# An attention and mixture-of-experts kernel: scores by pairs of key blocks with half passes, and some loads and stores begun by another engine

## The chip, the cores and the metric

The kernel runs on one core of a Trainium2 chip. The core has five engines that run their own instruction lists in order: TensorE (PE in the rows; its weight loads are listed as PEld), VectorE (DVE), ScalarE (ACT), GpSimd (POOL) and SyncE (SP), which here only begins DMA transfers. The metric is the device time of one execution in microseconds (us); smaller is better. For the kernel before, the median of three runs is 4315.48 us (4313.22 to 4316.8).

## The reference

Eight samples of 3072 rows go through three steps:

```
scores = z @ z.T / S                       # z: 3072 x 64 for each sample
out    = u * (max(scores, 0) ** 2 @ v)     # v, u: 3072 x 256
h      = out @ w_in                        # 24576 rows, 256 -> 1024
ln     = layernorm(h * softmax(h)) * g_ln
x      = ln @ w_out                        # 1024 -> 256
e      = argmax(x @ w_gate)                # one of 8 experts for each row
y      = gate * (max(x @ w1[e], 0) @ w2[e])
```

All of it is wanted in float32. The kernel splits float32 numbers into a high part that the matmul takes exactly (`fp32r`) and a low part, and sums the products high·high, high·low and low·high: three passes for each product.

## The kernel before, in words

**Chunks, blocks, slots.** A sample is cut into six chunks of 512 query rows (j = 0 to 5; 48 chunks in all) and 24 blocks of 128 keys. One slot of the program handles one key block of one chunk: six passes (two halves of the value width, three products each) accumulate `o<-ah,vw` and `o<-al,vw` in `pe_av` (the helper `mm3`, lines 108 to 110). Scores run four slots ahead (`LA`). The matrix z·zᵀ is symmetric, so a score block that an earlier chunk of the sample has computed is fetched from DRAM (`get`, tiles `sym<-kept`) in place of being computed; the six chunks of a sample compute 24, 20, 16, 12, 8 and 8 blocks, 88 in all, 704 over the eight samples.

**Scores.** z has 64 columns, so its transpose fills 64 of 128 partitions, and the tile `zw` holds the high part on partitions 0 to 63 and the low part on 64 to 127. The tile `zv` is the same with the halves exchanged (`swap_z`: two GpSimd instructions for each chunk). `pe_scores` runs two full passes over 128 partitions into one of two PSUM buffers `s`: zw·zw (line 426) and zw·zv (line 427). Together these are all four products. ACT then makes `r` (relu, line 432), `a` (square, line 437) and `ah` (line 442), DVE makes `al` (line 447).

**Between the slots.** A finished chunk goes through w_in (`h`, `blk_h`), softmax and statistics, and a transposition by 32x32 blocks on DVE (`pb`, line 531) that is written to DRAM (`blk_put`, `moved<-pb`, line 540) and read back (`blk_get`, `pT<-moved`, line 546) to finish it; then w_out (`yp<-gw,pth`), routing on POOL and DVE, and an indirect DMA by POOL that sorts the rows by expert (`sorted_rows<-y,pi`, line 663). At the end the expert stage takes units of 512 or 256 sorted rows (`load_x`, `load_w`, `g`, `y`).

**What sets the order.** The order is written out by hand: `at(slot, fn, ...)` puts a step into a slot, and the last loop runs the slots. Each engine runs its instructions in that order. All DMA transfers are begun by SP, except the sorted rows and the outputs (indirect, by POOL) and the loads of u for the chunks j = 4 and 5 (`load_u`).

**The start.** Eight blocks of w_in and w_out come as 64-bit floats and are converted by integer work on DVE and POOL (`prep_w`, stepped by `step_w`); `WS` is the distance in slots between two of these blocks and `W0` the first slot. The chunks' z and v are loaded by `load_z` and `load_v`, prepared by `prep_z`, `prep_v`, `prep_v_lo`.

Of the kernel before, what the change touches and what calls it, by code (L numbers as in the profile page):

```python
# [33 lines left out]
def attention_moe_kernel(ctx, tc, u, v, z, w_in, w_out, g_ln, w_gate, w1, w2, out):  # L34
# [16 lines left out]
    GA = 3  # L51
    NSYM = 8
    PD = 1
# [3 lines left out]
    TW = 8  # L57
    WS, W0, W1, W2 = 4, -11, 0, 2
    YT = 1
# [72 lines left out]
    with ExitStack() as st:  # L132
# [22 lines left out]
        def at(slot, fn, *args):  # L155
            events[slot].append((fn, args))
# [12 lines left out]
        x64, r64, gwt = t[:2], t[2], t[3]  # L169
        gw64 = mp.tile([P, F], F32, tag="p", name="gw64", bufs=1)[:, :CH].rearrange("p (m d) -> p m d", d=D)  # L170
        n_in = KD * F // CH
# [68 lines left out]
        def load_consts():  # L240
            nc.sync.dma_start(out=w_gate_sb, in_=w_gate.rearrange("(k p) e -> p k e", p=P))
            nc.sync.dma_start(out=g_sb, in_=g_ln.rearrange("(k p) -> p k", p=P))
            for h in range(HALF // P):
                nc.sync.dma_start(out=xs[DUMMY + h * P:DUMMY + (h + 1) * P], in_=pad_row)
# [18 lines left out]
        z_raw, v_raw, u_raw = {}, {}, {}  # L263
        z_t, z2_t, v_t = {}, {}, {}

# [4 lines left out]
        def load_z(c):  # L270
            t = raw.tile([P, CH], F32, tag="zd", name="zd")
            src = rows(z, c).rearrange("(a i) (b j) -> b i a j", i=32, j=32)
            for x in range(4):
                nc.sync.dma_start(out=t[x * 32:(x + 1) * 32].rearrange("i (a j) -> i a j", j=32), in_=src[x % 2])
            z_raw[c] = t
# [5 lines left out]

        def prep_z(c):
            zt = z_raw.pop(c)
            up_, low = slice(0, DZ), slice(DZ, 2 * DZ)
            w = zp.tile([P, CH], F32R, tag="zw", name="zw")
            A.activation(out=w, in_=zt, func=AF.Copy)
            if c == 0:
                w2_ = zp.tile([P, CH], F32R, tag="zv", name="zv", bufs=2)
                A.activation(out=w2_, in_=zt, func=AF.Copy)
                z2_t[c] = w2_  # L290
            V.tensor_tensor(out=w[low], in0=zt[low], in1=w[low].bitcast(F32), op=ALU.subtract)
            if c == 0:
                V.tensor_tensor(out=w2_[up_], in0=zt[up_], in1=w2_[up_].bitcast(F32), op=ALU.subtract)
            z_t[c] = w

        def swap_z(c):

            w = zp.tile([P, CH], F32R, tag="zv", name="zv", bufs=2)
            G.tensor_scalar(out=w[:DZ], in0=z_t[c][DZ:], scalar1=1.0, scalar2=1.0, op0=ALU.mult, op1=ALU.mult)
            G.tensor_scalar(out=w[DZ:], in0=z_t[c][:DZ], scalar1=1.0, scalar2=1.0, op0=ALU.mult, op1=ALU.mult)  # L300
            z2_t[c] = w

        def load_v(c, h):
            t = raw.tile([P, 2, D], F32, tag="vr", name="vr", bufs=2)
            nc.sync.dma_start(out=t, in_=rows(v, c).rearrange("(h r p) d -> h p r d", h=2, p=P)[h])
            v_raw[c, h] = t
# [113 lines left out]

        def pe_scores(n):
            c = n // NKB
            _, _, k, r = block(n)
            w = z_t[(c // NCB) * NCB + k][:, r * P:(r + 1) * P]
            s = ps_s.tile([P, CH], F32, tag="s", name="s")
            T.matmul(out=s, lhsT=w, rhs=z_t[c], start=True, stop=False)
            T.matmul(out=s, lhsT=w, rhs=z2_t[c], start=False, stop=True)  # L427
            s_t[n] = s

# [107 lines left out]
        def blk_put(c, t):  # L537
            w = pb_t.pop((c, t))
            for x in range(4):
                nc.sync.dma_start(out=moved[t][:, x], in_=w[x * 32:(x + 1) * 32])  # L540

# [222 lines left out]
        def take(name):  # L764
# [7 lines left out]
            elif name == "xT1":  # L772
                xT_t[1] = own(mp, "xt", [P, 2, KD, CH])
            elif name == "hT":
                t = [own(zp, "zw", [P, CH]) for _ in range(NCB)]
                t += [own(zp, "zv", [P, CH], bufs=2) for _ in range(2)]
                hT_b.extend((t[i], t[i + 1]) for i in range(0, len(t) - 1, 2))
                o_b.extend(own(ap, "a", [P, CH], F32, bufs=NA).rearrange("p (r d) -> p r d", d=D) for _ in range(2))
            elif name == "out":
                t = own(mp, "p", [P, F], F32)  # L780
                o_b.extend(t[:, i * CH:(i + 1) * CH].rearrange("p (r d) -> p r d", d=D) for i in range(2))
            elif name == "set1":
                c = [own(raw, "zd", [P, CH], F32)]
                t = own(raw, "ur", [P, KD, CH], F32)
                c += [t[:, 0], t[:, 1]]
                c += [own(ap, "r", [P, CH], F32) for _ in range(2)] + [own(ap, "a", [P, CH], F32, bufs=NA), own(mp, "sym0", [P, CH], F32)]
                c += [own(mp, f"sym{i}", [P, CH], F32) for i in (1, 2)]
                c = [t.bitcast(F32R) for t in c]
                c += [own(ap, "ah", [P, CH], bufs=4) for _ in range(4)]
                c += [own(ap, "al", [P, CH], bufs=3) for _ in range(3)]  # L790
                for i, k in enumerate(("w1h", "w1l", "w2h", "w2l")):
                    w_set[1, k] = c[4 * i:4 * i + 4]

        x_row = {}

        def load_x(i, part=None):

            n = units[i]
            if not part:
                x_row[i] = nc.sync.value_load(row_i[0:1, i:i + 1], min_val=0, max_val=DUMMY - (n if n == FULL else 0))  # L800
                xr_t[i] = xrow.tile([P, KD * CH], F32, tag="x", name="x")
# [6 lines left out]
            for dst, x in todo if part is None else todo[3 * part:3 * part + 3]:  # L808
                nc.sync.dma_start(out=dst, in_=x)

        def load_w(i, k):
            e = nc.sync.value_load(expert_i[0:1, i:i + 1], min_val=0, max_val=NE - 1)
            w = (w1 if k == 1 else w2)[ds(e, 1)].rearrange("o (k p) f -> p (o k) f", p=P)
            t = raw_w[f"raw{k}"].rearrange("p (k f) -> p k f", f=w.shape[2])
            nc.sync.dma_start(out=t, in_=w)

# [99 lines left out]
        for c in range(NCHUNK):  # L916
# [3 lines left out]
            if b == 0:  # L920
                base = 4 * j - Z0
                zload = base - 5 + (j > 0)
                vload = 4 * j - V0
                at(base, turn_z, c)
            else:
# [10 lines left out]
            for h in range(2):  # L936
                step, wait = (3, 5) if b else (2, 2)
                at(vload + step * h, load_v, c, h)
                at(vload + step * h + wait, prep_v, c, h)
                at(vload + step * h + wait + (b > 0), prep_v_lo, c, h)  # L940
            for x in range(4):
# [36 lines left out]
        for b in range(n_in + n_out):  # L978
            for i in range(14):
                at(WS * b + W0 + max(W2 - b, 0) + i, step_w, b)  # L980
        at(W0 + 4, load_consts)
        at(4 * (n_in + n_out) + W1, prep_sum)

# [127 lines left out]
```

## Time and profile before

| what | value |
|---|---|
| median of three runs | 4315.48 us |
| profiled execution: its own time | 4313.29 us |
| profiled execution: span | 4311.6 us, mean granted clock 0.995 |
| PE busy | 4231.3 us (98%), 23458 matmuls |
| DVE, ACT, POOL busy | 3197.2, 2800.7, 1200.7 us |
| DMA queues' share of 16 engines | 72.9% hardware queue, 4.4% POOL's queue |

The span goes from the first to the last instruction; the device time has 1.7 us around it. Busy times of engines overlap. A matmul counts as busy from its start to its modelled end, and the next starts before that end, so 98% does not mean that the array streams 98% of the time: the distance from one start to the next tells that. A score block is worth two passes; a slot with its score is worth eight, and the slots of j = 0 all have a score. In the windows below the first pair of numbers is the stretch; the DMA share is the mean busy share of 16 DMA engines.

### The profile page before, as it was taken

Reading aid. Unit: us, or ns where it says so; the run is one execution under the profiler, and the core shown is the slowest. Engines: PE = TensorE matmul, PEld = TensorE weight load, DVE = VectorE, ACT = ScalarE, POOL = GpSimd, SP = SyncE. Lnnn points to the kernel's source line nnn. Section 1 sums busy time; section 2 is a strip of 40 time slices with the busy share of each in tenths; the row PEclk is TensorE's granted clock in tenths of the full one; section 3 lists DMA queues with packets and bytes.
Section 4 is the critical chain, followed back from the end, with each engine's and each line's share of the span. In section 5 each row is a group of like instructions: output and inputs, shape, how many; then the busy total and the mean of one; then the engine's idle time right before and its main releaser. Section 6 shows DMA issues by size and latency. Waiting matters only on the chain.

```text
span 4311.6 us, 74509 instructions
## 1 busy us (share of the span) xinstructions
PE 4231.3 (98%) x23458; PEld 3664.3 (85%) x23458; DVE 3197.2 (74%) x5624; ACT 2800.7 (65%) x5184; POOL 1200.7 (28%) x2486
## 2 busy tenths in 40 slices
PE   7999999999999999999999999999899999999999
PEld 5888888888888888888888888888788999999998
DVE  8777787777778787877877787777666656655686
ACT  6766776776677677667767766775444444444565
POOL 5023223322322332232233233323222111111111
PEclk9999999999999999999999999999999999999999
DMA  5799789889978988897898899789755655555575
GB/s 150 169 171 167 184 174 163 178 177 175 159 192 173 163 180 180 172 161 192 172 164 183 173 174 162 186 166 165 145 147 150 156 145 134 145 137 146 155 212 170
DMA packets 2465549, 719.23 MB, mean 167 GB/s; under 512 B 2261117, under 2 KB 2351485, under 8 KB 2465152
## 3 DMA queue, kind: packets, MB, share of 16 engines
q1 hardware_dynamic: 2441952, 654.93, 72.9%
q0 software_dynamic: 23200, 59.55, 4.4%
q8 instruction: 183, 3.00, 0.3%
q14 instruction: 214, 1.75, 0.1%
HBM read 442.46 MB, written 273.49 MB: 166 GB/s over the span
## 4 chain that ended last, share of the span: by engine, by line
PE 75%; DMA 7%; SPq 7%; DVE 6%; issue 2%; ACT 2%; POOL 0%; DVEq 0%; POOLq 0%; ACTq 0%
PE o L109 10%; PE o L108 10%; PE o L110 9%; SPq L410 4%; PE y L109 3%; PE y L108 3%; PE y L110 3%; PE g L108 3%; PE yp L108 3%; PE g L109 3%; PE yp L110 3%; PE yp L109 3%; PE h L494 3%; PE h L495 3%; PE h L498 3%; PE g L110 3%
## 5 line engine op out<-in xcount | busy, mean ns | idle before, releaser
L109 PE MATMUL o<-al,vw 128*128 128x512 f32 x2304 | 912.8, 396 | 26.6 <-DVE al L447 26.0
L108 PE MATMUL o<-ah,vw 128*128 128x512 f32 x2304 | 910.4, 395 | 3.0 <-DVE ut L471 2.8
L110 PE MATMUL o<-ah,vw 128*128 128x512 f32 x2304 | 900.7, 391 | 0.0
L442 ACT ACTIVATE ah<-a 128x512 fp32r<-128x512 f32 x832 | 526.0, 632 | 201.1 <-DVE a L416 77.1
L432 ACT ACTIVATE r<-s 128x512 f32<-128x512 f32 x704 | 415.3, 590 | 344.8 <-PE s L427 327.1
L447 DVE TENSOR_TENSOR al<-a,ah 128x512 fp32r<-128x512 f32 x832 | 575.5, 692 | 1.0
L109 PEld LDWEIGHTS o<-al,vw 128*128 128x128 f32 x2304 | 434.6, 189 | 122.0 <-DVE al L447 44.1
L110 PEld LDWEIGHTS o<-ah,vw 128*128 128x128 f32 x2304 | 434.9, 189 | 93.8
L108 PEld LDWEIGHTS o<-ah,vw 128*128 128x128 f32 x2304 | 434.7, 189 | 88.0 <-issue 2.7
L105 DVE TENSOR_TENSOR ptl<-pT,pth 128x512 fp32r<-128x512 f32 x384 | 264.2, 688 | 267.5 <-ACT pth L104 266.5
L108 PE MATMUL yp<-gw,pth 128*128 128x264 f32 x1536 | 440.1, 286 | 13.5 <-ACT pth L104 13.5
L437 ACT ACTIVATE a<-r 128x512 f32<-128x512 f32 x704 | 437.6, 622 | 12.9 <-DVE al L447 11.2
L110 PE MATMUL yp<-gw,ptl 128*128 128x264 f32 x1536 | 438.8, 286 | 0.9 <-DVE ptl L105 0.9
L869 ACT ACTIVATE zw_x<-g 128x512 fp32r<-128x512 f32 (+1 forms) x350 | 183.0, 523 | 393.6 <-PE g L110 390.0
L109 PE MATMUL yp<-gw,pth 128*128 128x264 f32 x1536 | 438.5, 285 | 0.0
L870 DVE SCALAR_TENSOR_TENSOR zw_x<-g,zw_x 128x512 fp32r<-128x512 f32 (+1 forms) x350 | 208.3, 595 | 266.2 <-ACT zw_x L869 260.9
L663 POOL DMA_INDIRECT sorted_rows<-y,pi x192 | 206.5, 1076 | 426.0 <-DMA sorted_rows<-y,pi 375.4
L104 ACT ACTIVATE pth<-pT 128x512 fp32r<-128x512 f32 x384 | 237.8, 619 | 123.4 <-DMA pT<-moved 123.3
L108 PEld LDWEIGHTS yp<-gw,pth 128*128 128x128 f32 x1536 | 289.7, 189 | 30.2 <-ACT pth L104 15.5
L495 PE MATMUL h<-w_in,xt 128*128 128x512 f32 x768 | 304.7, 397 | 0.0
L494 PE MATMUL h<-w_in,xt 128*128 128x512 f32 x768 | 304.4, 396 | 0.0
L109 PEld LDWEIGHTS yp<-gw,pth 128*128 128x128 f32 x1536 | 290.7, 189 | 14.4
(276 smaller groups left out, 10641.7 us busy)
## 6 DMA issues: line engine op xcount, KB each, us to landing
vw_x<-in_moe_w SPq DMA_DIRECT2D x124, 1024.0 KB
sym<-kept SPq DMA_DIRECT2D x1792, 64.0 KB
moved<-pb SPq DMA_DIRECT2D x768, 128.0 KB
pT<-moved SPq DMA_DIRECT2D x768, 128.0 KB
kept<-sym SPq DMA_DIRECT2D x320, 256.0 KB
kept<-a SPq DMA_DIRECT2D x128, 256.0 KB
vr<-in_v SPq DMA_DIRECT2D x96, 256.0 KB
x<-sorted_rows SPq DMA_DIRECT2D x328, 64.0 KB
```

What stands on the lines that cost most here:

```text
L104: A.activation(out=hi, in_=src, func=AF.Copy)
L105: V.tensor_tensor(out=lo, in0=src, in1=hi.bitcast(F32), op=ALU.subtract)
L108: T.matmul(out=out, lhsT=lh, rhs=rh, start=start, stop=False, **kw)
L109: T.matmul(out=out, lhsT=lh, rhs=rl, start=False, stop=False, **kw)
L110: T.matmul(out=out, lhsT=ll, rhs=rh, start=False, stop=stop, **kw)
L432: A.activation(out=r, in_=s_t.pop(n), func=AF.Relu)
L437: A.activation(out=a, in_=r_t.pop(n), func=AF.Square)
L442: A.activation(out=h, in_=a_t[n], func=AF.Copy)
L447: V.tensor_tensor(out=l, in0=a_t[n], in1=ah_t[n].bitcast(F32), op=ALU.subtract)
L494: T.matmul(out=h[:, fs], lhsT=w[:, 0, kd, ts_], rhs=w_in_t[0][:, kd, fs], start=(kd == 0), stop=False)
L495: T.matmul(out=h[:, fs], lhsT=w[:, 0, kd, ts_], rhs=w_in_t[1][:, kd, fs], start=False, stop=False)
L870: V.scalar_tensor_tensor(out=lo, in0=h, scalar=0.0, in1=hi.bitcast(F32), op0=ALU.max, op1=ALU.subtract)
```

## The change

Three things change, and a few slots and buffer counts with them.

First, scores. `prep_z` and `swap_z` lay z out differently: in `zw` even key blocks have the high part above and the low part below, odd blocks the other way round. For the queries of a chunk there are two tiles, `zh` with the high part in both halves and `zl` with the low part in both halves (eight GpSimd instructions of 64 x 256 for each chunk in place of two of 64 x 512). `pe_scores` takes two key blocks that follow one another among the computed ones, one even and one odd: for each a full pass zw·zh (high·high and low·high), and then for each a pass over only 64 partitions, zw[half]·zl[half] (high·low). The even block uses partitions 0 to 63 and the odd one 64 to 127. The product low·low is left out. Both `s` buffers belong to one pair.

Second, POOL begins some DMA transfers in place of SP: v for later samples (`load_v`, chunks j < 4: 28 chunks, two each), the writes of `pb` for chunks j = 3 and 4 (`blk_put`: 15 chunks, 16 each, which fall into the slots of j = 4 and 5), and the first two units of the experts (`load_x`, `load_w`). ACT begins two of the four loads of the very first z.

Third, slots: the weight blocks at the start stand 5 slots apart in place of 4 (`WS`, `W0`), both halves of the first v are loaded at one slot, the constants and the filling of `sorted_rows`' dummy rows come later, `NSYM` goes from 8 to 7.

```diff
-    NSYM = 8
+    NSYM = 7
-    WS, W0, W1, W2 = 4, -11, 0, 2
+    WS, W0, W1, W2 = 5, -10, 0, 2
...
         def prep_z(c):
...
-                w2_ = zp.tile([P, CH], F32R, tag="zv", name="zv", bufs=2)
-                A.activation(out=w2_, in_=zt, func=AF.Copy)
-                z2_t[c] = w2_
-            V.tensor_tensor(out=w[low], in0=zt[low], in1=w[low].bitcast(F32), op=ALU.subtract)
+                zh, zl = q_tiles(c)
+                A.activation(out=zh, in_=zt, func=AF.Copy)
+            for i, half in enumerate((low, up_)):
+                x, y = [t.rearrange("p (r two k) -> p r two k", two=2, k=P)[half, :, i] for t in (zt, w)]
+                V.tensor_tensor(out=y, in0=x, in1=y.bitcast(F32), op=ALU.subtract)
...
+        def q_tiles(c):
+            zq_t[c] = [zp.tile([P, CH], F32R, tag=k, name=k, bufs=2) for k in ("zh", "zl")]
+            return zq_t[c]
+
         def swap_z(c):
 
-            w = zp.tile([P, CH], F32R, tag="zv", name="zv", bufs=2)
-            G.tensor_scalar(out=w[:DZ], in0=z_t[c][DZ:], scalar1=1.0, scalar2=1.0, op0=ALU.mult, op1=ALU.mult)
-            G.tensor_scalar(out=w[DZ:], in0=z_t[c][:DZ], scalar1=1.0, scalar2=1.0, op0=ALU.mult, op1=ALU.mult)
-            z2_t[c] = w
+            zw = z_t[c].rearrange("p (r two k) -> p r two k", two=2, k=P)
+            for low, w in enumerate(q_tiles(c)):
+                w = w.rearrange("p (r two k) -> p r two k", two=2, k=P)
+                for half in range(2):
+                    for odd in range(2):
+
+                        at_ = odd ^ low
+                        G.tensor_scalar(out=w[half * DZ:(half + 1) * DZ, :, odd],
+                                        in0=zw[at_ * DZ:(at_ + 1) * DZ, :, odd],
+                                        scalar1=1.0, scalar2=1.0, op0=ALU.mult, op1=ALU.mult)
 
         def load_v(c, h):
...
-            nc.sync.dma_start(out=t, in_=rows(v, c).rearrange("(h r p) d -> h p r d", h=2, p=P)[h])
+            eng = G if c >= NCB and c % NCB < NCB - 2 else nc.sync
+            eng.dma_start(out=t, in_=rows(v, c).rearrange("(h r p) d -> h p r d", h=2, p=P)[h])
...
         def pe_scores(n):
+            if n in s_t:
+                return
             c = n // NKB
-            _, _, k, r = block(n)
-            w = z_t[(c // NCB) * NCB + k][:, r * P:(r + 1) * P]
-            s = ps_s.tile([P, CH], F32, tag="s", name="s")
-            T.matmul(out=s, lhsT=w, rhs=z_t[c], start=True, stop=False)
-            T.matmul(out=s, lhsT=w, rhs=z2_t[c], start=False, stop=True)
-            s_t[n] = s
+            zh, zl = zq_t[c]
+            pair = [n, next(i for i in range(n + 1, (c + 1) * NKB) if not is_kept(i))]
+            ws = []
+            for i, x in enumerate(pair):
+                _, _, k, r = block(x)
+                assert r % 2 == i
+                ws.append(z_t[(c // NCB) * NCB + k][:, r * P:(r + 1) * P])
+                s_t[x] = ps_s.tile([P, CH], F32, tag="s", name="s")
+            for x, w in zip(pair, ws):
+                T.matmul(out=s_t[x], lhsT=w, rhs=zh, start=True, stop=False)
+            for i, (x, w) in enumerate(zip(pair, ws)):
+                half = slice(i * DZ, (i + 1) * DZ)
+                T.matmul(out=s_t[x], lhsT=w[half], rhs=zl[half], start=False, stop=True)
...
         def blk_put(c, t):
             w = pb_t.pop((c, t))
+
+            eng = G if NCB - 3 <= c % NCB < NCB - 1 and c < NCHUNK - 2 else nc.sync
             for x in range(4):
-                nc.sync.dma_start(out=moved[t][:, x], in_=w[x * 32:(x + 1) * 32])
+                eng.dma_start(out=moved[t][:, x], in_=w[x * 32:(x + 1) * 32])
...
+        def dma_of(i):
+
+            return G if i < 2 else nc.sync
...
+                if c == 0:
+                    step, wait = 0, 6
                 at(vload + step * h, load_v, c, h)
...
-        at(W0 + 4, load_consts)
-        at(4 * (n_in + n_out) + W1, prep_sum)
+        at(1, load_consts)
+        at(2 * NKB, fill_dummy)
+        at(WS * (n_in + n_out) + W1 - 1, prep_sum)
```

How the instructions stand on PE in the first slots of the second sample, before (`o` is the accumulated output, `s` a score tile, `h` the product with w_in):

```order
L108 MATMUL o_4617<-ah,vw 128x512
L109 MATMUL o_4617<-al,vw 128x512
L110 MATMUL o_4617<-ah,vw 128x512
L108 MATMUL o_4621<-ah,vw 128x512
L109 MATMUL o_4621<-al,vw 128x512
L110 MATMUL o_4621<-ah,vw 128x512
L426 MATMUL s<-zw 128x512
L427 MATMUL s<-zv,zw 128x512
```

The same stretch of PE's list in the changed kernel:

```order
L108 MATMUL o_4672<-ah,vw 128x512
L109 MATMUL o_4672<-al,vw 128x512
L110 MATMUL o_4672<-ah,vw 128x512
L108 MATMUL o_4676<-ah,vw 128x512
L109 MATMUL o_4676<-al,vw 128x512
L110 MATMUL o_4676<-ah,vw 128x512
L453 MATMUL s<-zh,zw 128x512 x2
L456 MATMUL s<-zl,zw 128x512 x2
```

Where two passes stood behind every block, four stand behind every second one: two over 128 partitions (line 453) and two over 64 (line 456, 64 partitions each).

On POOL, in the slots of the chunk j = 4 of the first sample, before (`pi` is where the rows go, `vv` a step of the normalization):

```order
L330 DMA ur<-in_u 32x16x32 x2
L659 CAST pi<-pf 128x4
L663 DMA sorted_rows<-y,pi 198656x264 x4
L580 TENSOR_SCALAR vv<-se 128x4
L581 TENSOR_TENSOR vv<-vv 128x4
L582 TENSOR_SCALAR vv<-vv 128x4
L583 TENSOR_TENSOR vv<-vv,q 128x4
L584 TENSOR_SCALAR vv<-vv 128x4
L299 TENSOR_SCALAR zv<-zw 64x512
L300 TENSOR_SCALAR zv<-zw 64x512
```

The same place on POOL in the changed kernel:

```order
L347 DMA ur<-in_u 32x16x32 x2
L689 CAST pi<-pf 128x4
L570 DMA moved<-pb 32x1024 x4
L693 DMA sorted_rows<-y,pi 198656x264 x3
L570 DMA moved<-pb 32x1024 x4
L693 DMA sorted_rows<-y,pi 198656x264
L610 TENSOR_SCALAR vv<-se 128x4
L611 TENSOR_TENSOR vv<-vv 128x4
L612 TENSOR_SCALAR vv<-vv 128x4
L613 TENSOR_TENSOR vv<-vv,q 128x4
L614 TENSOR_SCALAR vv<-vv 128x4
L315 TENSOR_SCALAR zh<-zw 64x2x128 x4
```

Two groups of four writes of `pb` now stand before and among the sorting DMAs, ahead of `vv` and of the exchange of z; four more instructions for `zl` follow the four shown for `zh`.

On ACT, the first instructions of the program before (`vw<-vr` prepares v, `r<-s` is the first relu):

```order
L286 ACT_TABLE_LOAD
L286 ACTIVATE zw<-zt 128x512
L289 ACTIVATE zv<-zt 128x512
L314 ACTIVATE vw<-vr 128x512 x2
L432 ACTIVATE r<-s 128x512
```

On SP, the first transfers before:

```order
L274 DMA zd<-in_z 32x16x32 x4
L181 DMA raw_142<-in_moe_w_in 128x1024
L305 DMA vr<-in_v 128x2x256
L274 DMA zd<-in_z 32x16x32 x4
L241 DMA w_gate_sb<-in_moe_w_gate 128x2x8
L242 DMA g_sb<-in_moe_g_ln 128x8x1
L244 DMA sorted_rows<-pad_row 128x264 x2
L305 DMA vr<-in_v 128x2x256
```

And in the changed kernel:

```order
L278 DMA zd<-in_z 32x16x32 x2
L322 DMA vr<-in_v 128x2x256 x2
L182 DMA raw_142<-in_moe_w_in 128x1024
L278 DMA zd<-in_z 32x16x32 x4
L322 DMA vr<-in_v 128x2x256
```

The second load of v goes from the fifteenth place on SP (rows with x4 and x2 counted singly) to the fourth; ACT's list keeps both preparations of v ahead of the first relu.

## Rows read from the trace of the kernel before

**Rows 1.** The page, part 1: busy us, share of the span, instructions.
```profile
PE 4231.3 (98%) x23458; PEld 3664.3 (85%) x23458; DVE 3197.2 (74%) x5624; ACT 2800.7 (65%) x5184; POOL 1200.7 (28%) x2486
```
**Rows 2.** Windows: chunks j = 0, 4 and 5 of the fifth sample.
```profile
core 0: us, PE busy (x) PEld busy (x) DVE busy (x) ACT busy (x) POOL busy (x), PEclk, DMA share, GB/s
1544.90:1611.50 66.60, 66.60 (x337) 56.29 (x336) 55.40 (x92) 54.91 (x101) 22.14 (x48) 1.00 0.82 198
...
1800.60:1860.30 59.70, 59.70 (x308) 50.74 (x308) 43.77 (x77) 37.82 (x68) 20.73 (x50) 1.00 0.93 164
1860.30:1922.70 62.40, 61.72 (x314) 51.71 (x314) 46.74 (x82) 40.82 (x72) 27.07 (x56) 1.00 1.00 171
```
**Rows 3.** Timeline of PE and PEld around one score block: start, us, engine, line.
```profile
1002.63 0.39 PE L110 MATMUL o<-ah,vw 128*128 128x512 f32 x1
1002.86 0.39 PE L426 MATMUL s<-zw 128*128 128x512 f32 x1
1003.09 0.39 PE L427 MATMUL s<-zv,zw 128*128 128x512 f32 x1
...
1002.86 0.19 PEld L427 LDWEIGHTS s<-zv,zw 128*128 128x128 f32 x1
```
**Rows 4.** Four transposes of 128 columns back to back, and their durations (ns).
```profile
90.99 0.60 PE L225 MATMUL tp<-ident,gw 128*128 128x128 f32 x4
...
L225 PE MATMUL tp<-ident,gw x16: 270/272/329, 68.4 to 101.4; 128*128 128x128 f32 x16
```
**Rows 5.** PE's waits from 100 to 2960 us: us, times, longest.
```profile
PE o L109 <- DVE al L447: 8.7, 19, 0.8
```
**Rows 6.** PE's waits from 0 to 100 us.
```profile
PE o L109 <- DVE al L447: 12.7, 7, 3.8
PE s L426 <- ACT r L432: 8.1, 5, 5.0
```
**Rows 7.** Windows at the start: 20 to 40 us, and the next 40 us after the first 100.
```profile
20.00:40.00 20.00, 12.50 (x41) 9.63 (x41) 18.05 (x24) 12.11 (x22) 11.49 (x9) 0.91 0.49 107
...
100.00:140.00 40.00, 39.74 (x193) 32.99 (x192) 31.02 (x50) 32.17 (x59) 1.41 (x3) 1.00 0.58 138
```
**Rows 8.** DVE's weight work, 0 to 100 us: first and last of six lines.
```profile
L193 DVE TENSOR_SCALAR cu<-raw 128x512 int32<-128x512 int32 x8 | 8.1, 1012 | 3.1 <-POOL t L204 3.1
...
L198 DVE TENSOR_SCALAR cu<-cu 128x512 int32<-128x512 int32 x8 | 4.7, 591 | 0.1
```
**Rows 9.** Timeline of ACT at the start; idle time before, and what ended it.
```profile
8.02 0.63 ACT L314 ACTIVATE vw<-vr 128x512 fp32r<-128x512 f32 x1 [0.98 <-DMA vr<-in_v]
13.48 0.63 ACT L314 ACTIVATE vw<-vr 128x512 fp32r<-128x512 f32 x1 [4.83 <-DMA vr<-in_v]
14.01 0.58 ACT L432 ACTIVATE r<-s 128x512 f32<-128x512 f32 x1
```
**Rows 10.** A relu and the next score block, at the start of a sample.
```profile
1538.68 0.58 ACT L432 ACTIVATE r<-s 128x512 f32<-128x512 f32 x1
...
1538.27 0.39 PE L426 MATMUL s<-zw 128*128 128x512 f32 x1
```
**Rows 11.** POOL: DMA issues of u, and the exchange of z (min/median/max ns).
```profile
L330 POOL DMA_DIRECT2D ur<-in_u x128 | 85.0, 675 | 0.1
...
L300 POOL TENSOR_SCALAR zv<-zw x47: 614/620/1177, 77.4 to 2967.8; 64x512 fp32r<-64x512 f32 x47
```
**Rows 12.** Timeline of SP's queue in a chunk j = 4: start, us, count.
```profile
1801.50 4.28 SPq L410 DMA_DIRECT2D sym<-kept  x8
1805.88 1.83 SPq L540 DMA_DIRECT2D moved<-pb  x4
1807.75 5.82 SPq L410 DMA_DIRECT2D sym<-kept  x8
```
**Rows 13.** DVE's waits on POOL in the fifth sample, 1544.9 to 1922.7 us.
```profile
DVE vw L321 <- POOL vw L316: 1.2, 1, 1.2
```
**Rows 14.** Waits from 2980 to 3200 us: ACT's longest, and PE's from 2960.
```profile
ACT pth L104 <- DMA pT<-moved: 30.9, 7, 7.7
...
PE yp L108 <- ACT pth L104: 13.5, 4, 5.9
PE g L108 <- DVE zw_x L870: 6.9, 3, 2.8
```

More of the change, by code (lines that the diff above doesn't have):

```diff
@@ L169, in attention_moe_kernel @@
         x64, r64, gwt = t[:2], t[2], t[3]
-        gw64 = mp.tile([P, F], F32, tag="p", name="gw64", bufs=1)[:, :CH].rearrange("p (m d) -> p m d", d=D)
+        gw64 = mp.tile([P, 4, RW], F32, tag="y", name="gw64", bufs=2).rearrange("p t w -> p (t w)")[:, :CH]
+        gw64 = gw64.rearrange("p (m d) -> p m d", d=D)
         n_in = KD * F // CH
@@ L242, in load_consts, with fill_dummy @@
             nc.sync.dma_start(out=g_sb, in_=g_ln.rearrange("(k p) -> p k", p=P))
+        def fill_dummy():
             for h in range(HALF // P):
@@ L263, in attention_moe_kernel @@
         z_raw, v_raw, u_raw = {}, {}, {}
-        z_t, z2_t, v_t = {}, {}, {}
+        z_t, zq_t, v_t = {}, {}, {}
         def rows(x, c):
@@ L273, in load_z @@
             for x in range(4):
-                nc.sync.dma_start(out=t[x * 32:(x + 1) * 32].rearrange("i (a j) -> i a j", j=32), in_=src[x % 2])
+                eng = A if c == 0 and x >= 2 else nc.sync
+                eng.dma_start(out=t[x * 32:(x + 1) * 32].rearrange("i (a j) -> i a j", j=32), in_=src[x % 2])
             z_raw[c] = t
@@ L775, in take @@
                 t = [own(zp, "zw", [P, CH]) for _ in range(NCB)]
-                t += [own(zp, "zv", [P, CH], bufs=2) for _ in range(2)]
+                t += [own(zp, "zh", [P, CH], bufs=2) for _ in range(2)]
                 hT_b.extend((t[i], t[i + 1]) for i in range(0, len(t) - 1, 2))
@@ L799, in load_x @@
             if not part:
-                x_row[i] = nc.sync.value_load(row_i[0:1, i:i + 1], min_val=0, max_val=DUMMY - (n if n == FULL else 0))
+                x_row[i] = dma_of(i).value_load(row_i[0:1, i:i + 1], min_val=0, max_val=DUMMY - (n if n == FULL else 0))
                 xr_t[i] = xrow.tile([P, KD * CH], F32, tag="x", name="x")
@@ L808, in load_x @@
             for dst, x in todo if part is None else todo[3 * part:3 * part + 3]:
-                nc.sync.dma_start(out=dst, in_=x)
+                dma_of(i).dma_start(out=dst, in_=x)
         def load_w(i, k):
-            e = nc.sync.value_load(expert_i[0:1, i:i + 1], min_val=0, max_val=NE - 1)
+            e = dma_of(i).value_load(expert_i[0:1, i:i + 1], min_val=0, max_val=NE - 1)
             w = (w1 if k == 1 else w2)[ds(e, 1)].rearrange("o (k p) f -> p (o k) f", p=P)
             t = raw_w[f"raw{k}"].rearrange("p (k f) -> p k f", f=w.shape[2])
-            nc.sync.dma_start(out=t, in_=w)
+            dma_of(i).dma_start(out=t, in_=w)
         def split_w(i, k, s):
@@ L923, in attention_moe_kernel @@
                 vload = 4 * j - V0
+                if j == 0:
+                    vload = base - 5
                 at(base, turn_z, c)
@@ L937, in attention_moe_kernel @@
                 step, wait = (3, 5) if b else (2, 2)
+                if c == 0:
+                    step, wait = 0, 6
                 at(vload + step * h, load_v, c, h)
-                at(vload + step * h + wait, prep_v, c, h)
-                at(vload + step * h + wait + (b > 0), prep_v_lo, c, h)
+                at(vload + step * h + wait + h * (c == 0), prep_v, c, h)
+                at(vload + step * h + wait + h * (c == 0) + (b > 0), prep_v_lo, c, h)
             for x in range(4):
```

2 lines of the change are left out of this document (1 added, 1 removed).

## The prediction

> **What bounds the kernel now.** I read the page first: PE is busy 98% of the span, the next engine, DVE, 74% [rows 1]. Busy is not proof, so I looked at the distances between starts and at what PE waits for. In the timeline a pass of 512 columns starts every 0.23 us (0.227 to 0.23 in the rows shown), whatever stands before and behind it: output, score, score [rows 3]. PE's waits over the 2860 us from 100 to 2960 us are led by 8.7 us for `al` [rows 5], a third of a per cent. So in the attention stage PE streams without a gap, and a pass that is gone is worth 227 ns. The waits lie at two ends: the first 100 us (12.7 us for `al`, 8.1 us for a relu [rows 6]) and the passage to the experts, where PE waited 13.5 us for `pth` and 6.9 us for the first expert units [rows 14].
>
> The windows of the fifth sample say how near the others are. With j = 0, DVE has 55.4 and ACT 54.9 of 66.6 us; with j = 4 and 5 DVE is at 44 to 47 of some 61, but the DMA engines stand at 0.93 and 1.00 [rows 2], and SP's queue in such a chunk issues back to back, 0.46 to 0.73 us for each transfer [rows 12]. j = 5 is the one chunk of a sample in which PE is not full (61.72 of 62.40): there transfers end last.
>
> **The change: passes.** 704 blocks make 352 pairs (44 for each sample: 12, 10, 8, 6, 4, 4). Before, a pair is four passes, 908 ns. After, it is two full passes and two of 64 partitions. A half pass streams the same 512 columns, so alone it costs a pass; the gain stands on the two running at once. No row shows a half pass. Bounds for the cost of the two halves together:
> - Lower: 227 ns, exactly one pass. The pair saves 227.
> - 227 + 108: a weight load starts when the matmul before it starts (1002.86 for both [rows 3]), and 4-byte weights take 108 ns: four transposes end 0.60 us after the first start, one lasts 272 ns, so they start (600 - 272)/3 = 109 ns apart although each streams only 128 columns [rows 4]. If the second half's weights are loaded only once the first half runs, it starts 108 later. The pair saves 119.
> - 454: one after the other. The pair saves nothing.
> - Beyond: a loss, if going from 128 to 64 partitions and back empties the array (a rival below).
>
> I take 227 + 20. The second half's weights go into partitions that the first half does not use, so both loads can run under the last full pass: 2 x 108 = 216 of 227. Nothing in the rows forbids it, but nothing proves it either. On this the Trainium skill ("TensorE: Matmul & The Clock Gate", Part 3) says that matmuls on different row groups run at once and start about 4 ns apart; by that the halves would cost 231, and the sum below would come out 5 us lower. No run here shows it.
>
> Saved per pair: 908 - 454 - 247 = 207 ns. It doesn't count everywhere. In the 12 pairs of the first chunk DVE is the bound (18.05 of 20 us against PE's 12.50 [rows 7]). In the 32 pairs of j = 5 transfers are; I count none of those either. 352 - 12 - 32 = 308 pairs x 207 ns = **-63.8 us** (bounds: 340 x 227 = -77, and 0 or a loss).
>
> **A wait that comes in.** Both `s` buffers now belong to one pair, so its second full pass needs the relu of the block just before the pair, where each block needed only that of the block before last. At the start of a sample ACT is behind: the relu of the previous block ends at 1538.68 + 0.58 = 1539.26, the score block starts at 1538.27 [rows 10]. The second full pass would want to start at 1538.50 and would wait 0.76 us. Behind it stands everything on PE. For the seven later samples, with one such wait or two in each, I take 7 x 0.85 = **+6 us** (0 to +12). Elsewhere ACT keeps up, and the relu of a second block is early.
>
> **The start.** DVE's weight work is six lines of eight instructions, the largest 8.1 us and the smallest 4.7 [rows 8], by the mean of these 6 x 6.4 = 38 us, 4.8 us a block. With 5 slots between blocks, the eighth block's DVE work falls behind slot 24 and about half of the seventh's; some 1.5 x 4.8 = 7 us leave the stretch that DVE bounds, for one in which DVE has 31.02 of 40 and PE is full [rows 7]. Beside it, the first relu runs at 14.01 although its scores are long done: it stands on ACT behind the preparation of the second half of v, which idled 4.83 us for its load [rows 9]. That load goes from the fifteenth transfer to the fourth. Part of the 4.83 is then DVE's again, so I take 2. Together **-9 us** (0 to -13). `prep_z` costs DVE the same elements in two instructions; the later constants are covered by some 30 slots until their first use.
>
> **POOL and SP.** The exchange of z takes eight instructions in place of two. One of 64 x 512 takes 620 ns [rows 11]; one of half the length takes 310 to 620, so eight take 2.5 to 5 us in place of 1.2. It is issued five slots (some 13 us at 2.6 us a slot) before its first score, which covers it; without the cover PE would wait up to 4 us a chunk. In the slots of j = 5, POOL gets 16 writes of `pb`, about 7 loads of v and the longer exchange: at 675 ns a transfer [rows 11] that is 23 x 0.675 + 2.5 = 18 us on top of 27 of 62 [rows 2]. It fits, and DVE's only wait on POOL in the whole sample is 1.2 us [rows 13], so POOL has slack in front of DVE. What stands behind a write that waits for `pb` is the next sorting DMA, `vv` (DVE waits for it next) and the exchange. SP loses 16 transfers of some 0.46 us [rows 12] in these chunks. What that can give is bounded by PE's 8.7 us of waits for `al`, and DMA engines at 1.00 do the same bytes as before; I take 0 for all of this (-9 to +30, the upper end as a rival).
>
> **The passage to the experts.** 22 transfers of the first two units go from SP to POOL, about 10 us of SP's queue at 0.46. There ACT waited 30.9 us for `pT`, which SP fetches, and PE 13.5 us behind that [rows 14]; but part of it is the chain of the last chunk itself. On POOL the same transfers stand behind the last sorting DMAs, which they have to wait for anyway. I take **-4 us** (-15 to +5).
>
> **Sum.** Against the profiled execution's own 4313.3 us: -63.8 + 6 - 9 - 4 = 4242.5. That execution stands 2.2 us below the median of the runs, so I expect a median of **4245 us**, 1.6% less.
>
> **Rivals.**
> 1. *The second half starts a weight load late* (227 + 108): 308 x 119 = 36.7 in place of 63.8. For it: every load in the trace starts with the matmul ahead, never earlier. Against: never are two loads for different partitions in line. 4272 us.
> 2. *The array empties at each change of size.* A pass lasts 0.39 and the next starts after 0.23, so 0.16 us of each overlap with the next [rows 3]. If a change between 128 and 64 partitions has to wait for that, a pair pays it twice: 454 + 247 + 2 x 163 = 1027 against 908, +119 ns x 340 pairs = +40 us, and 4313.3 + 40 + 6 - 9 - 4 + 2.2 = **4349 us: slower**. It decides from the point where the two changes cost more than 207 ns together. The rows can't speak against it, since all passes here have 128 partitions. The Trainium skill ("TensorEngine Tiling (Array Packing)", Key Properties) states that changing the tiling mode drains TensorE; no run here shows it so far.
> 3. *The change doesn't do what it says*: halves run one after the other. No pass is saved: 4313.3 + 6 - 9 - 4 + 2.2 = 4308 us.
> 4. *POOL is late.* POOL runs its list in order, so a write that waits for `pb` holds up `vv` and with it DVE, `al` and PE. For: 45 us of work in some 60 plus waits. Against: rows 13's 1.2 us. 15 chunks x 2 us = +30: 4275 us.
>
> **Chances.** Forecast 0.45 (its own range 4225 to 4265), late weight load 0.22, emptied array 0.13, no overlap 0.08, POOL late 0.12. Two executions of this kernel differ by less than 0.2% (about 9 us), so that is what a measurement can tell from no change: faster is below 4307. The forecast, rivals 1 and 4 lie there wholly, and a small part of rival 3: 0.80. Within 0.2%: the rest of rival 3, 0.07. Slower: 0.13. A range of 8 in 10 leaves out rival 2 and the lowest end, where all bounds meet: 4222 to 4310 us.
>
> **What would show it.** Right: the two rows of line 456 start less than 0.03 us apart, and the next pass 0.23 to 0.26 after the first of them; PE's first full stretch begins some 9 us earlier. Rival 1: 0.11 apart. Rival 3: 0.23 apart. Rival 2: a gap of 0.39 ahead of line 456 and behind it. POOL late: DVE's waits on POOL in j = 4 and 5 in place of 1.2 us. The wait for the relu: `s` waiting on line 460 at every sample's start. Most of all the forecast falls if the start distance around line 456 is not that of one pass.

## The result, and the profile after

| kernel | median (us) | ratio to before, 95% interval |
|---|---|---|
| before | 4315.79 | 1 |
| changed | 4364.46 (4363.26 to 4367.36) | 1.0114, 1.0098 to 1.013 |

The change makes the kernel 49 us slower; I had forecast 4245 us, and 4349 for the rival in which the array empties. The changed kernel's page, part 1, answers to [rows 1]:

```profile
PE 4289.5 (98%) x23458; PEld 3576.2 (82%) x23458; DVE 3198.6 (73%) x5672; ACT 2791.1 (64%) x5184; POOL 1487.3 (34%) x3086
```

PE has as many matmuls as before, is as full as before, and is busy 58 us longer. POOL has 287 us more. The place to look is again a score block. This is PE's timeline of the changed kernel around the end of a pair (start, us, engine, line), the answer to [rows 3]:

```profile
1009.86 0.39 PE L453 MATMUL s<-zh,zw 128*128 128x512 f32 x1
1010.18 0.50 PE L456 MATMUL s<-zl,zw 64*128 64x512 f32 x2
1010.61 0.39 PE L108 MATMUL yp<-gw,pth 128*128 128x264 f32 x1
1010.84 0.28 PE L109 MATMUL yp<-gw,pth 128*128 128x264 f32 x1
1010.96 0.29 PE L110 MATMUL yp<-gw,ptl 128*128 128x264 f32 x1
```

And PEld's, the weight loads, in the same stretch (the idle time before a load and what ended it in brackets):

```profile
1010.18 0.19 PEld L456 LDWEIGHTS s<-zl,zw 64*128 64x128 f32 x2 [0.35 <-issue]
1010.61 0.19 PEld L108 LDWEIGHTS yp<-gw,pth 128*128 128x128 f32 x1 [0.25 <-issue]
1010.72 0.19 PEld L109 LDWEIGHTS yp<-gw,pth 128*128 128x128 f32 x1
```

Three things are to be seen. Both half passes together last 0.50 us: they do run side by side; the records put their starts 3 ns apart (median; 2 to 5 ns in the 350 of 352 pairs that stand whole in the trace). The Trainium skill ("TensorE: Matmul & The Clock Gate", Part 3) gives about 4 ns for it; the trace agrees.

Second, the first half starts 0.32 after the last full pass in place of 0.23, and the pass behind starts 0.43 after the halves.

Third, look at PEld. In [rows 3] a load starts together with the matmul *ahead* of its own. Here the load of line 456 starts with its own matmul (1010.18), and so does that of `yp` (1010.61): it was not pulled ahead over the change of size. The first pass after each change therefore lasts about 0.11 longer (`yp` 0.39 against 0.28 of the next), and the one behind it comes 0.11 later: 1010.61 to 1010.84 is 0.23, where the next distance is 0.12.

PEld's longest waits from 100 to 2960 us say that this is so everywhere in this kernel (an `issue` wait of at most 0.4 us, 319 times; in all 352 pairs the loads on both sides start at most 5 ns ahead of their own pass):

```profile
PEld s L456 <- issue: 112.3, 319, 0.4
```

The median distances between starts are, in ns: full to full 227; into the half size 318; half to half 3; from there to the next full pass 428. Over the 264 pairs of the second to seventh sample, the mean distances differ from the usual one by +90 (into the half size), -225 (half to half), +199 (out of it) and +104 (the one behind that). So going in and out costs 90 + 199 + 104 = 393 ns, the overlap gives 225, a pair loses **168 ns** (1076 in place of 908), and 352 pairs lose 59 us.

The other answers. PE's waits from 100 to 2960 us in the changed kernel, beside [rows 5]:

```profile
PE o L109 <- DVE al L475: 10.3, 16, 2.6
...
PE s L453 <- ACT r L460: 0.5, 1, 0.5
```

Its windows at the start, beside [rows 7]:

```profile
20.00:40.00 20.00, 14.71 (x48) 9.62 (x46) 18.51 (x27) 12.65 (x24) 9.90 (x8) 0.96 0.58 130
...
100.00:140.00 40.00, 37.16 (x181) 28.50 (x180) 33.89 (x55) 28.81 (x55) 8.67 (x12) 1.00 0.58 143
```

PE gets 2.2 us more from 20 to 40, and 2.6 us less from 100 to 140. DVE's waits on POOL in the fifth sample, beside [rows 13] with its 1.2:

```profile
DVE vw L338 <- POOL vw L333: 6.6, 2, 4.2
DVE yi L618 <- POOL vv L614: 3.5, 2, 1.8
```

### The profile page after: what moved, and what is told of

It is laid out like the page before. It is cut to its first block, busy times and chain, and to the rows that moved or that the text cites. A ratio compares the mean times of both kernels' runs of the same rounds, so it can differ in the third digit from the quotient of the medians.

```text
span 4363.4 us, 75363 instructions
## 1 busy us (share of the span) xinstructions
PE 4289.5 (98%) x23458; PEld 3576.2 (82%) x23458; DVE 3198.6 (73%) x5672; ACT 2791.1 (64%) x5184; POOL 1487.3 (34%) x3086
## 3 DMA queue, kind: packets, MB, share of 16 engines
q1 hardware_dynamic: 2402016, 603.39, 67.8%
## 4 chain that ended last, share of the span: by engine, by line
PE 80%; DMA 7%; DVE 3%; issue 2%; SPq 2%; POOL 1%; ACT 1%; DVEq 0%; POOLq 0%; ACTq 0%
PE o L108 11%; PE o L109 11%; PE o L110 10%; PE yp L108 4%; PE h L522 4%; PE yp L109 4%; PE yp L110 4%; PE h L526 4%; PE h L523 4%; PE s L453 3%; PE y L109 3%; PE y L108 3%; PE y L110 3%; PE s L456 3%; PE g L108 3%; PE g L109 3%
## 5 line engine op out<-in xcount | busy, mean ns | idle before, releaser
L109 PEld LDWEIGHTS o<-al,vw 128*128 128x128 f32 x2304 | 435.4, 189 | 100.2 <-DVE al L475 24.2
L108 PE MATMUL yp<-gw,pth 128*128 128x264 f32 x1536 | 451.9, 294 | 8.2 <-ACT pth L104 8.1
L109 PE MATMUL yp<-gw,pth 128*128 128x264 f32 x1536 | 439.4, 286 | 0.0
L538 DVE TENSOR_REDUCE nm<-h 128x1 f32<-128x1024 f32 x192 | 234.5, 1221 | 149.5 <-PE h L526 140.2
L470 ACT ACTIVATE ah<-sym 128x512 fp32r<-128x512 f32 x320 | 201.3, 629 | 211.1 <-PE o L110 124.9
L108 PEld LDWEIGHTS yp<-gw,pth 128*128 128x128 f32 x1536 | 291.4, 190 | 46.5 <-issue 25.9
L522 PE MATMUL h<-w_in,xt 128*128 128x512 f32 x768 | 321.2, 418 | 0.0
L523 PE MATMUL h<-w_in,xt 128*128 128x512 f32 x768 | 304.2, 396 | 0.0
```

The lines of the kernel that those rows point to most:

```text
L108: T.matmul(out=out, lhsT=lh, rhs=rh, start=start, stop=False, **kw)
L109: T.matmul(out=out, lhsT=lh, rhs=rl, start=False, stop=False, **kw)
L470: A.activation(out=h, in_=a_t[n], func=AF.Copy)
L522: T.matmul(out=h[:, fs], lhsT=w[:, 0, kd, ts_], rhs=w_in_t[0][:, kd, fs], start=(kd == 0), stop=False)
L523: T.matmul(out=h[:, fs], lhsT=w[:, 0, kd, ts_], rhs=w_in_t[1][:, kd, fs], start=False, stop=False)
L538: V.tensor_reduce(out=s["nm"][:, t:t + 1], in_=h, axis=AX.X, op=ALU.max, negate=True)
```

## Experiments: the half passes

The theory: each change of size costs about 197 ns (393 / 2), and this is the loss. The rivals: the halves do save what I forecast and the loss is elsewhere; or the price hangs on the pair, not on the change.

**All passes full.** The changed kernel with

```diff
-            for i, (x, w) in enumerate(zip(pair, ws)):
-                half = slice(i * DZ, (i + 1) * DZ)
-                T.matmul(out=s_t[x], lhsT=w[half], rhs=zl[half], start=False, stop=True)
+            for x, w in zip(pair, ws):
+                T.matmul(out=s_t[x], lhsT=w, rhs=zl, start=False, stop=True)
```

> The changed kernel with its low passes over all 128 partitions again (four full passes for a pair, low times low counted as before); nothing else differs. If each passage into and out of the half size costs what the trace after shows (pair 1076 ns against 908, 168 x 352 pairs = 59 us), this kernel takes 4364.5 - 59 = about 4305 us, a little less than before. If the half passes do save the 64 us forecast and the loss is elsewhere (POOL's list, the start, the slots), it takes 4364.5 + 64 = about 4428 us. If halves and full passes cost the same, 4364.

Measured 4317.54 us (ratio to before 1.0001, 0.999 to 1.0011). Full passes are 47 us faster than half passes. The rival's 4428 is out. The theory's price per pair stands (all distances around lines 453 and 455 are 227 here), but 12 of its 59 us don't arrive: a faster PE waits more. In the six samples from the second to the seventh, the starts that come over 50 ns late, those at the changes of size left out, add up to 23.4 us here and 12.7 in the changed kernel. And the rest of the change, which I had at -7, is worth +2; the second group of experiments is about that.

**Full, half, full, half.** The changed kernel with the passes of a pair in this order:

```diff
-            for x, w in zip(pair, ws):
-                T.matmul(out=s_t[x], lhsT=w, rhs=zh, start=True, stop=False)
             for i, (x, w) in enumerate(zip(pair, ws)):
                 half = slice(i * DZ, (i + 1) * DZ)
+                T.matmul(out=s_t[x], lhsT=w, rhs=zh, start=True, stop=False)
                 T.matmul(out=s_t[x], lhsT=w[half], rhs=zl[half], start=False, stop=True)
```

> The changed kernel with a pair's passes in the order full, half, full, half: the same products, but the halves no longer stand side by side and there are four changes of size in a pair in place of two. If the price lies in each change (396 ns for in and out), a pair takes 4 x 227 + 2 x 396 = 1700 ns against 1076: + 624 x 352 = + 220 us, 4584 us. If the price is one for each pair, whatever the order, only the overlap is lost: + 227 x 352 = + 80 us, 4444 us.

Measured 4565.75 us (ratio 1.0579, 1.0559 to 1.0598): 201 us above the changed kernel, where the price for each change gave 220 and the price for each pair 80. Its PE timeline:

```profile
1000.12 0.39 PE L454 MATMUL s<-zh,zw 128*128 128x512 f32 x1
1000.44 0.50 PE L455 MATMUL s<-zl,zw 64*128 64x512 f32 x1
1000.87 0.49 PE L454 MATMUL s<-zh,zw 128*128 128x512 f32 x1
1001.30 0.49 PE L455 MATMUL s<-zl,zw 64*128 64x512 f32 x1
1001.72 0.39 PE L108 MATMUL yp<-gw,pth 128*128 128x264 f32 x1
1001.95 0.28 PE L109 MATMUL yp<-gw,pth 128*128 128x264 f32 x1
```

Every change shows the same: about 0.43 between starts that were 0.23, once the pass ahead is itself the first after a change (0.32 where it isn't, and 0.11 behind the last). The price lies in each change.

**Both halves on the same partitions.**

```diff
-                half = slice(i * DZ, (i + 1) * DZ)
+                half = slice(0, DZ)
```

> The changed kernel with both half passes of a pair on partitions 0 to 63; for the odd block this multiplies the wrong halves (low by low in place of high by low), so its scores lack the product high by low. If the two halves overlap in the changed kernel because they stand in different partitions, this order costs a pass more for each pair: 0.23 to 0.33 us (a pass, and a weight load if it can't run beside) x 352 = + 79 to + 117 us, 4443 to 4481 us. If the halves don't really overlap there and the 3 ns between their starts only hides a longer second one, no change: 4364 us.

Measured 4436.69 us (ratio 1.028, 1.0261 to 1.0299): 72 us above the changed kernel. The timeline has the second half 0.33 behind the first (the x2 row lasts 0.73):

```profile
1010.47 0.61 PE L453 MATMUL s<-zh,zw 128*128 128x512 f32 x2
1011.01 0.73 PE L456 MATMUL s<-zl,zw 64*128 64x512 f32 x2
1011.67 0.50 PE L522 MATMUL h<-w_in,xt 128*128 128x512 f32 x1
1012.01 0.40 PE L523 MATMUL h<-w_in,xt 128*128 128x512 f32 x1
```

At the median the halves now start 335 ns apart in place of 3, and the pass behind follows after 323 in place of 428, since the second half's load no longer stands in the open there: 227 ns more for a pair, one pass. That makes 80 us, of which 72 arrive (the 79 to 117 expected had left out that the way out gets shorter). So the overlap of the changed kernel is real and worth a pass. The saving that I forecast is there. It is smaller than the price of getting it.

**Three pairs of halves, no full pass.**

```diff
-            for x, w in zip(pair, ws):
-                T.matmul(out=s_t[x], lhsT=w, rhs=zh, start=True, stop=False)
-            for i, (x, w) in enumerate(zip(pair, ws)):
-                half = slice(i * DZ, (i + 1) * DZ)
-                T.matmul(out=s_t[x], lhsT=w[half], rhs=zl[half], start=False, stop=True)
+            for j, q in enumerate((zh, zl, zl)):
+                for i, (x, w) in enumerate(zip(pair, ws)):
+                    half = slice(i * DZ, (i + 1) * DZ)
+                    T.matmul(out=s_t[x], lhsT=w[half], rhs=q[half], start=j == 0, stop=j == 2)
```

> The changed kernel with all passes of a pair in the half size: three pairs of halves (high by high, high by low, high by low again), no full pass; the scores lack low by high and count high by low twice. One way in and one out for each pair, as in the changed kernel. If halves stream at a pass for each pair of them once the size is set, a pair takes 3 x 227 + 396 = 1077 ns, no change: 4364 us. If the weight load of each half stands in the open too (105 ns, as at the way out), + 2 x 105 x 352 = + 74 us: 4438 us.

Measured 4366.5 us (ratio 1.0117, 1.0099 to 1.0136), 2 us from the changed kernel. Its PE timeline (the six halves are the rows of line 455):

```profile
1000.50 0.39 PE L110 MATMUL o<-ah,vw 128*128 128x512 f32 x1
1000.82 0.50 PE L455 MATMUL s<-zh,zw 64*128 64x512 f32 x2
1001.15 0.63 PE L455 MATMUL s<-zl,zw 64*128 64x512 f32 x4
1001.71 0.50 PE L108 MATMUL o<-ah,vw 128*128 128x512 f32 x1
1002.05 0.40 PE L109 MATMUL o<-al,vw 128*128 128x512 f32 x1
```

Inside the half size two passes run at the price of one, weight loads hidden. What is paid is the way in (0.32, then 0.33) and the way out (0.32 behind the last pair, then 0.34): 4 x about 0.1 = 0.4 us, whatever stands between. The price belongs to the change, and work inside dilutes it.

## Experiments: the rest of the change

**The pairs alone.** The kernel before with pairs, half passes and the layout of `zh` and `zl`; transfers and start as before.

```diff
-            eng = G if c >= NCB and c % NCB < NCB - 2 else nc.sync
-            eng.dma_start(out=t, in_=rows(v, c).rearrange("(h r p) d -> h p r d", h=2, p=P)[h])
+            nc.sync.dma_start(out=t, in_=rows(v, c).rearrange("(h r p) d -> h p r d", h=2, p=P)[h])
```

(against the changed kernel; the other moves and the slots are undone in the same way)

> The kernel before with the pairs, half passes and the layout of zh and zl alone; SP begins all its transfers and the slots of the start are as before (the two buffers' counts and places go with it). If the changes of size are the whole loss, it stands as far above the kernel before as the changed kernel above the one with full passes: + 47, about 4363 us. If part of the loss comes from POOL's longer list or the start, it is less: 4340 us or below.

Measured 4374.51 us (ratio 1.0134, 1.0118 to 1.0149): +58, more than the 47 expected and about the 59 that 352 pairs lose by the distances. The rest of the change, which this kernel lacks, gains 10. Where the forecast's relu wait is, PE's waits from 100 to 2960 us in this kernel:

```profile
PE s L451 <- ACT r L458: 5.1, 8, 1.0
```

**The start alone.**

```diff
-    WS, W0, W1, W2 = 4, -11, 0, 2
+    WS, W0, W1, W2 = 5, -10, 0, 2
...
+                if c == 0:
+                    step, wait = 0, 6
```

> The kernel before with the changes of the start alone (WS and W0, the places of the first v, the constants, the dummy rows, ACT's two loads). By the prediction's term, - 9: 4306 us. By what the trace after shows (the first chunk 8.6 us shorter, the second 8.8 longer), the work only moves by one chunk: 4315 us, no change.

Measured 4315.19 us (ratio 0.9998, 0.9989 to 1.0007): nothing that can be measured. The first chunk takes 67.8 us in place of 76.5 and the second 67.7 in place of 62.6 (from the first value pass of one chunk to that of the next).

**The moves to POOL, together, then with the start.**

```diff
+            eng = G if NCB - 3 <= c % NCB < NCB - 1 and c < NCHUNK - 2 else nc.sync
             for x in range(4):
-                nc.sync.dma_start(out=moved[t][:, x], in_=w[x * 32:(x + 1) * 32])
+                eng.dma_start(out=moved[t][:, x], in_=w[x * 32:(x + 1) * 32])
```

(and the same for `load_v`, `load_x`, `load_w`)

> The kernel before with only the transfers of v, of pb and of the first two expert units begun by POOL in place of SP. By the prediction, - 4 at the passage to the experts: 4311 us. By its rival that POOL comes late, + 30: 4345 us. By the run with full passes, in which the start and these moves together came to + 2: 4315 us with the last sample some 4 us shorter and the end some 3 us longer.

> The kernel before with the start and the moves to POOL together, scores as before. If the terms add as predicted, - 13: 4302 us. If they are worth nothing, as the run with full passes has it, 4315 us; then the longer exchange of z (eight instructions) and the pairs' shared buffers cost nothing either.

Measured 4296.7 us (ratio 0.9949, 0.9935 to 0.9962) and, with the start, 4291.87 us (0.9944, 0.993 to 0.9958). So this half of the change is a gain of 19 to 24 us, more than any term that I gave it. **The second of them beats both kernels.** It also shows a gap: all passes full by pairs stands at 4317.5, 26 us above it, with the same start and moves. What differs is the layout with its exchange, the pairs' order and the buffer less.

**The parts of it.** Only the writes of `pb` (the diff above); only the first two expert units; the exchange of before done as eight instructions (each half written twice); `NSYM = 7`, the last two on top of start and moves.

```diff
-            G.tensor_scalar(out=w[:DZ], in0=z_t[c][DZ:], scalar1=1.0, scalar2=1.0, op0=ALU.mult, op1=ALU.mult)
-            G.tensor_scalar(out=w[DZ:], in0=z_t[c][:DZ], scalar1=1.0, scalar2=1.0, op0=ALU.mult, op1=ALU.mult)
+            for twice in range(2):
+                for x in range(2):
+                    for half in range(2):
+                        k, o = slice(x * CH // 2, (x + 1) * CH // 2), 1 - half
+                        G.tensor_scalar(out=w[half * DZ:(half + 1) * DZ, k], in0=z_t[c][o * DZ:(o + 1) * DZ, k],
+                                        scalar1=1.0, scalar2=1.0, op0=ALU.mult, op1=ALU.mult)
```

> The kernel before with only the writes of pb of the chunks j = 3 and 4 begun by POOL. The three moves together gave - 19, nearly all in the chunks j = 5 (63.56 to 61.19 us each). If it is SP's queue with these 16 writes that was late there, this move alone gives most of it: about 4300 us. If the loads of v did it, no change: 4316 us.

> The kernel before with only the first two expert units begun by POOL. By the prediction's term for the passage - 4: 4312 us. By the run with all three moves, in which the time from the last value pass to a tenth of the expert passes stayed at 110 us and the stretch behind the last pass grew by 3.3 us: 4316 to 4319 us.

> Start and moves to POOL with the scores of before, and the exchange of z as eight instructions of 64 x 256 (the two halves of before, cut in two and written twice). The kernel with full passes by pairs stands 26 us above start and moves alone, 21 of them in the chunks j = 5. If the longer exchange on POOL is the cause (v's preparation stands behind it), this kernel takes about 4310 us; if it is the pairs or the lost buffer, 4292 us.

> Start and moves to POOL with the scores of before, and seven buffers for the fetched score blocks in place of eight. If the lost buffer is the cause of the 26 us (transfers end last in j = 5), about 4310 us; if it is the exchange or the pairs, 4292 us.

The ratios are to the kernel before, run beside them (4316.0).

| kernel | median (us) | ratio, 95% interval |
|---|---|---|
| writes of `pb` alone | 4297.62 | 0.995, 0.9936 to 0.9963 |
| expert units alone | 4308.88 | 0.9981, 0.9972 to 0.999 |
| start, moves, eight instructions | 4325.99 | 1.0021, 1.0012 to 1.003 |
| start, moves, seven buffers | 4293.89 | 0.9946, 0.9932 to 0.9959 |

The writes of `pb` give 18. PEld's waits for `al` from 100 to 2960 us in the kernel before:

```profile
PEld o L109 <- DVE al L447: 20.8, 31, 1.2
```

and with the writes moved:

```profile
PEld o L109 <- DVE al L447: 1.0, 2, 0.6
```

PEld's row for `al` had 20.8 us where PE's had 8.7 [rows 5]: a late weight load is hidden in PE's view as long as the modelled end of the matmul ahead covers it. The gain, 18, is about the difference of PEld's rows (19.8). Counted by starts that come over 50 ns late (second to seventh sample), the passes that need `al` lose 14.8 us before and 3.6 with the writes moved.

What was late, by the trace, is what stands on SP. In a chunk j = 5 SP's transfers took 56.5 of 63.6 us to begin (mean of six samples), 7.0 of them for the 16 writes, and the fetches of score blocks stand behind these writes as in [rows 12]; with the writes moved it is 46.4 of 61.2. ACT waits less for the fetched blocks, before and with the writes moved (100 to 2960 us):

```profile
ACT ah L442 <- DMA sym<-kept: 99.9, 86, 2.8
```
```profile
ACT ah L442 <- DMA sym<-kept: 68.5, 56, 2.6
```

and PE is full in such a chunk, with the writes moved, where it had 61.72 of 62.40 us and a DMA share of 1.00 in [rows 2]:

```profile
1848.47:1909.53 61.06, 61.06 (x314) 51.89 (x314) 48.05 (x83) 40.15 (x73) 33.51 (x72) 1.00 0.94 169
```

Whether SP's time to begin the 16 transfers or their place in SP's queue was the cost isn't shown: the move takes both away.

The longer exchange costs 34 us; the lost buffer 2, within what can be told. POOL's timeline at the exchange in a chunk j = 5 shows how, first with eight instructions:

```profile
1907.98 0.51 POOL L594 TENSOR_SCALAR vv<-vv 128x4 f32<-128x4 f32 x1
1911.05 4.53 POOL L307 TENSOR_SCALAR zv<-zw 64x256 fp32r<-64x256 f32 x8 [2.56 <-DMA sorted_rows<-y,pi]
1915.67 0.63 POOL L325 TENSOR_SCALAR vw<-vr 128x512 fp32r<-128x512 f32 x1
```

and with two:

```profile
1887.02 0.62 POOL L303 TENSOR_SCALAR zv<-zw 64x512 fp32r<-64x512 f32 x1 [3.00 <-DMA sorted_rows<-y,pi]
1887.70 0.62 POOL L304 TENSOR_SCALAR zv<-zw 64x512 fp32r<-64x512 f32 x1
1888.41 0.63 POOL L321 TENSOR_SCALAR vw<-vr 128x512 fp32r<-128x512 f32 x1
```

Behind the exchange stands not a score but `vw`, the preparation of v that DVE waits for; behind DVE's half of it stands `al`, and behind that PE. Waits of DVE and of PE from 100 to 3000 us with eight instructions:

```profile
DVE vw L330 <- POOL vw L325: 43.7, 14, 4.1
```
```profile
PE o L109 <- DVE al L456: 22.4, 21, 3.0
```

With two they are these:

```profile
DVE vw L326 <- POOL vw L321: 28.5, 14, 2.4
```
```profile
PE o L109 <- DVE al L452: 5.0, 4, 2.2
```

Nearly all of these differences lie in the chunks j = 5 (mean of six samples, in us): before 63.56, writes of `pb` moved 61.17, start and moves 61.33, with eight instructions 65.71, all passes full by pairs 64.87, pairs alone 64.76, changed 64.09.

## Why the prediction was wrong

**The step that failed** is "I take 227 + 20. The second half's weights go into partitions that the first half does not use, so both loads can run under the last full pass: 2 x 108 = 216 of 227." No load goes under the last full pass: over a change of size none is pulled ahead, and the array waits besides. The halves cost 622 ns where I took 247 (1076 - 454): the forecast's -207 ns for a pair became +168. I had seen that every row had 128 partitions and chose the good end all the same, from an argument about partitions, not from a row.

**Rival 2** named the mechanism. The Trainium skill ("TensorEngine Tiling (Array Packing)", Key Properties) states its rule, that a change of the tiling mode drains the array; the trace agrees, with a start about 90 ns late at each change. The price was too low: 163 for each change, against 197. The 163 counted a drained pipeline alone; the trace has about 90 of that kind at each change (the start of line 456 that comes late) and about 105 for the load that then starts with its own pass. That 105 is about the 108 of the transposes [rows 4], which I had used in rival 1. That rival 2's 4349 came within 15 us of 4364 is partly luck: for all the rest of the change it had -7, where the runs show -24 and +26.

**The relu wait**, +6: it is 5.1 us in the kernel with the pairs alone, and 0.5 in the changed kernel. The mechanism is there; why the other changes take it away wasn't followed.

**The start**, -9: -0.9, with -5 to +3 as its interval. The chunks show why: what leaves the first falls into the second, 8.7 us shorter and 5.1 longer. I had counted DVE's work alone as moved; PE's transposes of these blocks and their waits move with it (in the changed kernel PE has 330 matmuls in the second chunk, 308 before). The 3.6 us that are left did not reach the end in this measurement.

**The passage**, -4: alone -7 (-12 to -4). In that kernel's trace PE waits 7.8 us for `pth` from 2960 to 3200 us in place of 13.5 [rows 14], though that execution was 9 us faster than the median of its runs.

**The chunks j = 5**, "transfers are" the bound: it was SP's list or queue and not the bytes, since PE is full there, with the same bytes moved, once POOL begins 16 of the writes.

**POOL and SP**, "I take 0 for all of this": this was two terms, and both were large. SP's 16 transfers gave 18 us, twice the -9 that I had drawn as the bound, since I took the bound from PE's waits and not from PEld's. And the exchange, which I covered with "issued five slots before its first score", has v's preparation behind it long before any score. Its length I had right (2.5 to 5 us; 4.53 in the row). Rival 4 had the direction: POOL's list holds DVE up, though by the exchange, not by the writes of `pb` themselves, which alone gave the 18.

The steps of the runs lead from before to the changed kernel: 4316.1 - 24.2 (start and moves) + 25.7 (layout, exchange, pairs' order) + 46.9 (half passes) = 4364.5. How much of the 25.7 the exchange has is not settled: with the old scores it costs 34, more than the whole step, and with SP's old list pairs and exchange together cost 58, no more than the 59 of the half passes. DVE's wait for `vw` (100 to 3000 us) points to where the exchange is dear. In the pairs alone, with the long exchange and SP's old list, it is

```profile
DVE vw L336 <- POOL vw L331: 10.4, 7, 1.5
```

It is 8.9 us with the writes of `pb` alone moved, 28.5 with all moves and the short exchange, 39.8 with all moves and the long one (all passes full). That points at the loads of v on POOL, but no run moved them alone, so it is not shown. The three moves together gave 19, two of them alone 18 and 7; the intervals are too wide to say whether the loads of v cost the difference.

## What to carry to other kernels

A half-size pass is not a small matmul but a change of the array: price the way in and out (here 393 ns) against what is saved inside (225 ns for each two halves); by these numbers (an estimate, not tried) two pairs of halves for each way in and out are the least that pays, and then by 57 ns. To bound what a late operand costs PE, read the waits of the weight loads, not those of the matmuls. Before calling a longer instruction on an idle engine covered, look for the next instruction in that engine's list that someone waits for, not for the first use of its own result.

## What the runs showed of the hardware

Weight loads were never pulled ahead over a change between 128 and 64 partitions, in either direction (352 pairs of the changed kernel), while inside the half size they were hidden after the first refill (0.33, then 0.24 between the starts of pairs of halves). The POOL copies of 64 x 256 took 403 ns at the median, against 620 for twice the length [rows 11]: cutting them in two costs 1.3 times as much. With the pauses between them it is more: in the chunks shown, eight take 4.53 us and two of twice the length 1.30, 1.7 times as much for the same data.
